# Stage 1 of a spectral mixing kernel: from one contraction over 128 rows to four row tiles of 32

## The chip, the cores and the metric

The kernel runs on one core of a Trainium2 chip. The metric is the device time in microseconds (us) of one execution; lower is better. The time of before is the median of three runs.

## The reference

Two global filters work on one image and a gate mixes them. The image `x` is 2048 rows by 1024 columns in bf16; each filter has weights for the real and the imaginary part, 2048 by 513.

```python
def _A_ref(x, w_r, w_i):
    B, S, D = x.shape                       # 1, 2048, 1024
    X = jnp.fft.rfft2(x.astype(jnp.float32), axes=(-2, -1))
    X = X * (w_r + 1j * w_i)
    return jnp.fft.irfft2(X, s=(S, D), axes=(-2, -1)).astype(jnp.bfloat16)
...
x = A_x
g = _sigmoid((x * gate_w).sum(-1, keepdims=True))
a = _A_ref(x, A_w_r, A_w_i)
b = _B_ref(x, B_w_r, B_w_i)
return g * a + (1 - g) * b
```

Both filters read the same `x`, so the forward transform is made once.

## The kernel before

The Fourier transforms are written as matrix products with constant tables, split so that each fits TensorE. The 2048 row indices are written as 64 n1 + 16 b + r, with n1 from 0 to 31, b from 0 to 3 (the residue that the change speaks of) and r from 0 to 15.

**Loads.** `x` is loaded with partition p holding the 16 rows 16 p to 16 p + 15, so partition p is 4 n1 + b and r is a place along the free dimension. Row blocks c = 0 to 3 hold four r each. `XPARTS` cuts them into nine DMAs: block 0 into one, one and two rows per partition, the others into two and two. All are issued on SP's queue, in order; two of the three loads of the table `M` stand between them (after blocks 0 and 1), the first `M` load goes by ACT's queue. Behind them, on SP's queue too, stand the table `F2`, the gate's weights (`GR`, eight rows of 128), `CK`, `SM`, and then all filter weights `w`, in six groups (w0 to w5; 44 DMAs with rows of 513 elements), and then `CL`, the tables for stage 5. The order within a queue is the order of the program text; every engine takes its own instructions in that order, and the class `Prog` turns the named reads and writes into semaphore waits.

**Fold.** VectorE adds and subtracts mirrored columns of x (`fold`, line 348) into `XF`, which holds two row blocks at a time.

**Stage 1** (`stage1`, matmul on line 387) is the first half of the transform down the columns. For each r, each half h, j and s there is one matmul with the folded x as the stationary operand and 256 columns of `M` (and of its negative, which `negate` writes on ACT or VectorE, lines 365 and 367) as the moving one. A column of M belongs to one b only, so three quarters of the table are zeros. The sums of one (h, j) of a row block fill two PSUM banks; they are evicted into `FT` by ACT (line 398) or, for two of them, VectorE (line 396), 1024 elements per partition at a time, for four r in a row.

**Stages 2 to 4**, for 16 steps: `fold3` on VectorE (line 443), the transform along the rows (`stage2`, lines 456 and 465), its eviction (line 471), the second half of the transform down the columns (`stage4`, line 482), its eviction (line 490), a DMA that swaps real and imaginary rows (`swap`), and the products with `w` on VectorE (`product`, line 505). The gate's spectrum is formed in between (line 518). **Stage 5** (line 614) and **stages 6 and 7** (lines 755 and 785) are the transforms back, with the gate, and the stores.

## Time and profile before

| | |
|---|---|
| time, median of 3 runs | 122.04 us (122.02 to 122.52) |
| the profiled execution | 122.14 us, span of its instructions 120.1 us |
| mean granted TensorE clock | 0.996 |
| TensorE busy | 114.1 us, 95% of the span |
| VectorE busy | 99.5 us, 83% |
| ACT busy | 99.0 us, 82% |
| DMA | 26.11 MB, 217 GB/s over the span |
| stage 1 matmuls, L387 | 128, starting from 5.0 to 20.3 us |
| stage 1 evictions on ACT, L398 | 15, starting from 8.3 to 21.1 us |
| stage 5 matmuls, L614 | 512, from 49.8 us on |

The page gives each engine's busy time; a matmul's end is modelled, so TensorE's share says little by itself. In the DMA row each digit is the busy share of the 16 DMA engines in one fortieth of the span. The chain of waits leads back from the last instruction to what released each step. In timelines a row is: start, duration, engine, line, operation, out<-in with shapes, count, and in brackets the idle time before it with what ended it.

### The profile page before, as it was taken

The page shows a single profiled execution, that of the slowest core. Times are in us where ns is not written, and L with a number is a line of the kernel's source. Part 1 is how long each engine was busy: PE and PEld are TensorE (multiplying, and loading weights), DVE is VectorE, ACT ScalarE, POOL GpSimd, SP SyncE. Part 2 cuts the span into 40 slices and gives each one's busy share as a digit, 9 for nine tenths or more (in the row PEclk, how much of TensorE's full clock was granted, in tenths as well). Part 3 has the DMA queues.
Part 4 walks back from the last instruction along what each step waited for, and adds up shares of the span by engine and source line. Part 5 has one row for each costly group of instructions (what it writes and reads, how often), then busy time and mean ns, then how long its engine had stood idle before and what let it go on. Part 6 is the DMA issues. An engine that isn't in the chain of part 4 may idle for free.

```text
span 120.1 us, 3690 instructions
## 1 busy us (share of the span) xinstructions
PE 114.1 (95%) x1556; PEld 95.9 (80%) x1556; DVE 99.5 (83%) x160; ACT 99.0 (82%) x119; POOL 38.4 (32%) x47
## 2 busy tenths in 40 slices
PE   6998999999999999999999999999999999999960
PEld 4676889787675675689999999999899979898630
DVE  0568999988999999999999949995695687787890
ACT  4249998999797999899999989999779868867710
POOL 1000010036575500000000000000029999999980
PEclk9999999999999999999999999999999999999998
DMA  2999999999999999832699500000000422434456
GB/s 84 328 394 421 415 331 366 349 350 352 361 369 364 360 370 368 321 137 85 162 392 394 199 0 5 0 5 0 0 5 8 158 96 93 175 124 160 160 222 215
DMA packets 17680, 26.11 MB, mean 217 GB/s; under 512 B 2112, under 2 KB 11072, under 8 KB 17664
## 3 DMA queue, kind: packets, MB, share of 16 engines
q1 hardware_dynamic: 16368, 23.00, 54.6%
q0 software_dynamic: 864, 2.36, 5.4%
q10 hardware_dynamic: 432, 0.52, 1.4%
q8 instruction: 12, 0.20, 0.7%
q14 instruction: 4, 0.03, 0.1%
HBM read 17.48 MB, written 4.19 MB: 180 GB/s over the span
## 4 chain that ended last, share of the span: by engine, by line
PE 59%; SPq 18%; DMA 9%; DVE 8%; issue 3%; ACT 1%; POOL 0%; DVEq 0%; POOLq 0%
PE PS L614 26%; SPq L290 18%; PE PS L785 14%; PE PS L755 11%; DMA WA<-in_B_w_i_dram 9%; DVE WA L505 3%; PE PS L304 3%; DVE WB L505 3%; PE PS L387 2%; DVE WA L796 1%; PE PS L561 1%; PE PS L482 1%; PE PS L588 1%; ACT WB L625 1%; DVEq L867 0%
## 5 line engine op out<-in xcount | busy, mean ns | idle before, releaser
L837 POOL TENSOR_TENSOR WA<-WA 128x512 bf16<-128x512 f32 x22 | 27.6, 1290 | 48.2 <-DVE WA L832 48.2
L614 PE MATMUL PS<-CL,WB 128*128 128x128 bf16 x256 | 31.8, 226 | 0.0
L614 PE MATMUL PS<-CL,WA 128*128 128x128 bf16 x256 | 31.7, 223 | 0.1
L614 PEld LDWEIGHTS PS<-CL,WB 128*128 128x128 bf16 x256 | 31.3, 145 | 0.3 <-DVE WB L505 0.2
L614 PEld LDWEIGHTS PS<-CL,WA 128*128 128x128 bf16 x256 | 31.3, 145 | 0.3 <-DVE WA L505 0.2
L625 ACT ACTIVATE WB<-PS 128x1024 bf16<-128x1024 f32 (+1 forms) x31 | 28.8, 1042 | 0.2 <-PE PS L614 0.2
L770 ACT ACTIVATE WA<-PS 128x1024 bf16<-128x1024 f32 (+1 forms) x16 | 15.8, 996 | 6.2 <-PE PS L755 6.1
L505 DVE TENSOR_TENSOR WB<-XF,WA 128x2048 bf16<-128x2048 bf16 (+2 forms) x14 | 19.3, 1384 | 1.0 <-ACT XF L490 0.5
L785 PE MATMUL PS<-FT,WA 128*128 128x256 bf16 (+1 forms) x132 | 19.3, 292 | 0.1
L505 DVE TENSOR_TENSOR WA<-MM,WA 128x2048 bf16<-128x2048 bf16 (+2 forms) x14 | 19.2, 1385 | 0.0
L482 PE MATMUL PS<-XF,CK 128*128 128x512 bf16 (+1 forms) x72 | 17.5, 356 | 0.2 <-ACT XF L490 0.2
L832 DVE TENSOR_TENSOR WA<-PS,WA 128x512 f32<-128x512 f32 x22 | 14.2, 686 | 4.2 <-PE PS L755 1.9
L471 ACT ACTIVATE XF<-PS 128x1024 bf16<-128x1024 f32 x16 | 16.7, 1052 | 1.1 <-PE PS L465 1.0
L490 ACT ACTIVATE XF<-PS 128x1024 bf16<-128x1024 f32 x14 | 14.7, 1050 | 1.4 <-PE PS L482 0.6
L387 PE MATMUL PS<-MM,XF 128*128 128x256 bf16 x128 | 15.4, 280 | 0.3 <-DVE XF L348 0.3
L387 PEld LDWEIGHTS PS<-MM,XF 128*128 128x128 bf16 x128 | 12.5, 100 | 3.3 <-DVE XF L348 1.4
L785 PEld LDWEIGHTS PS<-FT,WA 128*128 128x128 bf16 x132 | 12.3, 98 | 3.3 <-DVE WA L768 0.2
L290 POOL DMA_DIRECT2D MM<-XF x18 | 9.9, 550 | 14.3 <-PE PS L482 8.7
L398 ACT ACTIVATE FT<-PS 128x1024 bf16<-128x1024 f32 (+2 forms) x15 | 13.1, 1012 | 0.9 <-PE PS L387 0.9
L348 DVE TENSOR_TENSOR XF<-WB 128x512 bf16<-128x512 bf16 (+1 forms) x20 | 6.0, 366 | 5.9 <-DMA WB<-in_A_x_dram 5.9
L456 PEld LDWEIGHTS PS<-F,FT 128*128 128x128 bf16 x128 | 8.4, 98 | 3.1 <-ACT FT L398 0.2
L456 PE MATMUL PS<-F,FT 128*128 128x128 bf16 x128 | 10.2, 219 | 0.0
(77 smaller groups left out, 134.1 us busy)
## 6 DMA issues: line engine op xcount, KB each, us to landing
out_dram<-WA SPq DMA_DIRECT2D x14, 256.0 KB, 2.2
MM<-XF POOLq DMA_DIRECT2D x18, 128.0 KB, 5.3
WA<-in_A_x_dram SPq DMA_DIRECT2D x4, 512.0 KB, 8.3
FT<-c_U SPq DMA_DIRECT2D x1, 2048.0 KB, 8.5
MM<-XF SPq DMA_DIRECT2D x14, 128.0 KB, 3.2
WB<-in_A_x_dram SPq DMA_DIRECT2D x3, 512.0 KB, 5.9
WA<-in_A_w_r_dram SPq DMA_DIRECT2D x4, 256.5 KB, 5.8
WA<-in_A_w_i_dram SPq DMA_DIRECT2D x4, 256.5 KB, 6.2
```

Of the source, the lines that this page charges most:

```text
L290: return P.add(eng, lambda e: e.dma_start(dst, src), dma=name, **kw)
L387: P.add("pe", lambda e, o=o, lh=lh, rh=rh, s=s: e.matmul(o, lh, rh, start=(s == 0), stop=(s == 1)), r=[("xf", c % 2, q, h, s ^ j), ("M", c ...
L456: P.add("pe", lambda e, o=o, cs=cs, j=j, t=t, rh=rh: e.matmul(o, fblock(1 + cs, j, t), rh, start=(j == 0), stop=(j == 1)), r=[("F1a" if p ...
L471: P.add("act", lambda e: e.activation(dst, src, ACT.Copy), **kw)
L482: P.add("pe", lambda e, o=o, kind=kind, pm=pm, m=m, rh=rh: e.matmul(o, sl(CK, fbo(kind, pm, m), [(1, 128)]), rh, start=(m == 0), stop=(m = ...
L490: P.add("act", lambda e: e.activation(dst, src, ACT.Copy), **kw)
L505: P.add("dve", lambda e: e.tensor_tensor(out=at(sw), in0=sl(xt, xo + 64 * h0, [(0, 2), (128, 8 * ni), (1, 64 * n)]), in1=at(1), op=ALU.mul ...
L614: P.add("pe", lambda e, o=o, l0=l0, ab=ab: e.matmul(o, sl(WT[ab], l0, [(RWS[ab] // 2, 128)]), sl(CL, KIo[ab], [(1, 128)]), start=(ab == 0) ...
L625: P.add("act", lambda e: e.activation(dst, src, ACT.Copy), r=b, a=keys)
L770: P.add("act", lambda e, s=src, d=dst: e.activation(d, s, ACT.Copy), **kw)
L785: P.add("pe", lambda e: e.matmul(ps(col, [(1, n * 256)]), lh, rh, start=(k == 0), stop=(k == last)), r=[("Y", r), "DI"] + ["DJ"] * (full o ...
L837: P.add("pool", lambda e, s=s, op=op: e.tensor_tensor(out=ods(s, 0, 2), in0=pv[:, :, 0, :], in1=pv[:, :, 1, :], op=op), r=[("PQ", pk, 0), ...
```

## The change

The table `M` is stored without its zeros, [128, 512] in place of [128, 2048], with the four residues b as four groups of 32 partitions. The loads of x follow: partition 32 b + n1 now holds the rows 64 n1 + 16 b + r, so the source pattern of each load has a dimension of 4 outside one of 32. The nine DMAs keep their sizes and order; M is one DMA on ACT's queue and one negation on ACT.

A matmul of stage 1 then contracts over 32 partitions, with 64 moving columns, and there are four of them (g = 0 to 3), each in its own 32 rows of TensorE and its own PSUM bank, where one stood. A call of `stage1` fills four banks and evicts them in two evictions of 1024 elements. Row block 0 is evicted for two r at a time, with both h; the others for four r, one h at a time. The early key `F1a` goes, so `fold3` and `stage2` wait for `F1`.

```diff
-    C["M"] = M.reshape(128, 2048)
+    C["M"] = M.sum(-1).swapaxes(0, 1).reshape(128, 512)
...
-    xv = x2.rearrange("(p r) d -> p (r d)", r=16)
+    xsrc = lambda r, n: AP(x2.tensor, x2.offset + r * D, [[16 * D, 4], [64 * D, 32], [1, n * D]])
...
-    mload("act", 0, 1)
+    load("M", MM, 0, 512, cst["M"].ap(), eng="act", w=["M"])
     for c in range(4):
         t, o = xloc(c)
         for q0, n in XPARTS[c]:
-            dma("sp", f"x{c}{q0}", sl(t, o + q0 * 1024, [(1, n * 1024)]), xv[:, (4 * c + q0) * 1024:(4 * c + q0 + n) * 1024], w=[("x", c, q0)])
-        if c < 2:
-            mload("sp", 1 + c, 1 + c)
+            dma("sp", f"x{c}{q0}", sl(t, o + q0 * 1024, [(1, n * 1024)]), xsrc(4 * c + q0, n), w=[("x", c, q0)])
...
+    P.add("act", lambda e: e.activation(sl(MM, 512, [(1, 512)]), sl(MM, 0, [(1, 512)]), ACT.Copy, scale=-1.0), r=["M"], w=["NM"])
...
+    def stage1(c, q0, nq, hs, engs):
+
         nonlocal cnt
+        s0 = 4 * (cnt % 2)
+        cnt += 1
+        w = 128 * len(hs)
+        for q in range(q0, q0 + nq):
+            for h in hs:
                 for j in range(2):
+                    for s in range(2):
+                        for g in range(4):
+                            lh = sl(XF, (c % 2) * 4096 + q * 1024 + h * 512 + 256 * s + 128 * j, [(1, 128)], p0=32 * g, np_=32)
+                            rh = sl(MM, (4 * c + q) * 32, [(512 * s, 2), (1, 32)], p0=32 * g, np_=32)
+                            o = ps((s0 + g) * 512 + (q - q0) * w + (h - hs[0]) * 128 + j * 32, [(64, 2), (1, 32)])
                             P.add("pe", lambda e, o=o, lh=lh, rh=rh, s=s: e.matmul(o, lh, rh, start=(s == 0), stop=(s == 1)),
+                                  r=[("xf", c % 2, q, h, s ^ j), "M", "NM"], w=[bank(s0 + g)])
+        for g, eng in zip((0, 2), engs):
+            src = ps((s0 + g) * 512, [(512, 2), (1, w), (w, nq)])
+            dst = sl(FT, hs[0] * 8192 + 16 * g + 4 * c + q0, [(16, 2), (64, w), (1, nq)])
...
-    negate(0)
-    negate(1)
     folds(0)
     folds(1)
-    negate(2, 2, "dve")
-    stage1(0)
-    stage1(1)
+    for q0 in (0, 2):
+        stage1(0, q0, 2, (0, 1), ("act", "act"))
+    for hh in range(2):
+        stage1(1, 0, 4, (hh,), ("act", "act"))
...
-    stage1(2)
-    stage1(3)
+    for hh in range(2):
+        stage1(2, 0, 4, (hh,), ("act", "act"))
+    for hh in range(2):
+        stage1(3, 0, 4, (hh,), ("act", "dve"))
```

More of the change, by code (lines that the diff above doesn't have):

```diff
@@ L305, in bass_gated_mix__spectral_gfnet__spectral_gfnet__prompt_kernel @@
               r=["GRz"], w=[bank(7)])
-    def mload(eng, c0, n):
-        load(f"M{c0}", MM, c0 * 512, n * 512, cst["M"].ap()[:, c0 * 512:(c0 + n) * 512], eng=eng, w=[("M", c) for c in range(c0, c0 + n)])
-    mload("act", 0, 1)
+    load("M", MM, 0, 512, cst["M"].ap(), eng="act", w=["M"])
     for c in range(4):
@@ L359, in folds @@
             fold(c, q0, n, h)
-    def negate(c, n=1, eng="act"):
-        dst, src = sl(MM, 2048 + c * 512, [(1, n * 512)]), sl(MM, c * 512, [(1, n * 512)])
-        kw = dict(r=[("M", k) for k in range(c, c + n)], w=[("NM", k) for k in range(c, c + n)])
-        if eng == "dve":
-            P.add("dve", lambda e: e.tensor_scalar(out=dst, in0=src, scalar1=-1.0, scalar2=None, op0=ALU.mult), **kw)
-        else:
-            P.add("act", lambda e: e.activation(dst, src, ACT.Copy, scale=-1.0), **kw)
+    P.add("act", lambda e: e.activation(sl(MM, 512, [(1, 512)]), sl(MM, 0, [(1, 512)]), ACT.Copy, scale=-1.0), r=["M"], w=["NM"])
@@ L369, in bass_gated_mix__spectral_gfnet__spectral_gfnet__prompt_kernel @@
     cnt = 0
-    def stage1(c):
+    def stage1(c, q0, nq, hs, engs):
         nonlocal cnt
-        us = [(cnt + k) % 4 for k in range(4)]
-        cnt += 4
-        parts = XPARTS[c] if c == 0 else ((0, 4),)
-        for q0, n in parts:
-            for h in range(2):
-                for j in range(2):
-                    u = us[2 * h + j]
-                    for q in range(q0, q0 + n):
-                        r = 4 * c + q
-                        base = (c % 2) * 4096 + q * 1024 + h * 512
-                        o = ps(u * 1024 + q * 256, [(1, 256)])
-                        for s in range(2):
-                            lh = sl(XF, base + 256 * s + 128 * j, [(1, 128)])
-                            rh = sl(MM, r * 128, [(2048 * s, 2), (1, 128)])
-                            P.add("pe", lambda e, o=o, lh=lh, rh=rh, s=s: e.matmul(o, lh, rh, start=(s == 0), stop=(s == 1)),
-                                  r=[("xf", c % 2, q, h, s ^ j), ("M", c), ("NM", c)], w=[bank(2 * u + q // 2)])
-                    if q0 + n < 4:
-                        continue
-                    for m0, mn in ((0, 32), (32, 96)) if (c, h, j) == (3, 1, 1) else ((0, 128),):
-                        src = ps(u * 1024 + m0, [(128, 2), (1, mn), (256, 4)])
-                        dst = sl(FT, h * 8192 + j * 2048 + 16 * m0 + 4 * c, [(4096, 2), (16, mn), (1, 4)])
-                        kw = dict(r=[bank(2 * u), bank(2 * u + 1)], a=[("F1", h, j)] + [("F1a", h, j)] * (m0 == 0))
-                        if (c, h, j) in ((2, 1, 1), (3, 0, 1)):
-                            P.add("dve", lambda e, s=src, d=dst: e.tensor_copy(d, s), **kw)
-                        else:
-                            P.add("act", lambda e, s=src, d=dst: e.activation(d, s, ACT.Copy), **kw)
@@ new lines, in stage1 @@
+        for g, eng in zip((0, 2), engs):
+            src = ps((s0 + g) * 512, [(512, 2), (1, w), (w, nq)])
+            dst = sl(FT, hs[0] * 8192 + 16 * g + 4 * c + q0, [(16, 2), (64, w), (1, nq)])
+            kw = dict(r=[bank(s0 + g), bank(s0 + g + 1)], a=[("F1", h, j) for h in hs for j in range(2)])
+            if eng == "dve":
+                P.add("dve", lambda e, s=src, d=dst: e.tensor_copy(d, s), **kw)
+            else:
+                P.add("act", lambda e, s=src, d=dst: e.activation(d, s, ACT.Copy), **kw)
@@ L443, in fold3 @@
             P.add("dve", lambda e, dst=dst, src=src, op=op: e.tensor_tensor(out=dst, in0=src[0], in1=src[1], op=op),
-                  r=[("F1a" if i < 2 else "F1", cs, j) for cs in css for j in range(2)] + [("FR", i, j) for j in range(2)],
+                  r=[("F1", cs, j) for cs in css for j in range(2)] + [("FR", i, j) for j in range(2)],
                   w=[("E", i, cs, s) for cs in css] + [("FR", i - 2, s)] * (i > 1), a=["VD"] * (i == 1))
@@ L456, in stage2 @@
                         P.add("pe", lambda e, o=o, cs=cs, j=j, t=t, rh=rh: e.matmul(o, fblock(1 + cs, j, t), rh, start=(j == 0), stop=(j == 1)),
-                              r=[("F1a" if p < 2 else "F1", cs, j), "F2"], w=[bank(b0 + t % 2)])
+                              r=[("F1", cs, j), "F2"], w=[bank(b0 + t % 2)])
         if 1 in ab:
```

## The prediction, made before the changed kernel ran

> **What bounds the kernel now.** I read the page first, for where the transfers are dense, then the chain of waits, then the timelines of VectorE and TensorE for the first 50 us, and last the list of DMAs.

> ```profile
> DMA  2999999999999999832699500000000422434456
> GB/s 84 328 394 421 415 331 366 349 350 352 361 369 364 360 370 368 321 137 85 162 392 394 199 0 5 0 5 0 0 5 8 158 96 93 175 124 160 160 222 215
> ```

> A slice is 3.0 us. From the second slice to the fifteenth (3 to 45 us) the 16 DMA engines have no free time. Whatever holds up a transfer there holds up all that are queued behind it. The chain of waits leads through that stretch:

> ```profile
> 30.23 10.42 DMA WA<-in_B_w_i_dram
> 40.65 0.03 issue
> 40.68 0.02 DVEq L224
> 40.70 0.04 issue
> 40.74 1.61 DVE WB L505
> ```

> Before 30.23 us the chain runs through SP's queue, issue after issue (the w loads). So the filter weights (w, in six groups w0 to w5) set the pace up to 40.7 us. VectorE meets them just as they land:

> ```profile
> 31.24 2.38 DVE L505 TENSOR_TENSOR WB<-XF,WA 128x2048 bf16<-128x2048 bf16 x2 [0.26 <-DMA WA<-in_B_w_i_dram]
> ...
> 40.74 2.31 DVE L505 TENSOR_TENSOR WB<-XF,WA 128x4096 bf16<-128x4096 bf16 x1 [0.17 <-DMA WA<-in_B_w_i_dram]
> ```

> The first wait is for w2 (landed 31.14 us), the second for w3 (40.65 us). Slack at both is a fraction of a microsecond, and VectorE then works without a gap until stage 5. So a later w stream moves the end one for one. Ahead of w in SP's queue lie the nine loads of x:

> ```profile
> WA<-in_A_x_dram SPq DMA_DIRECT2D x4, 512.0 KB, 8.3
> WB<-in_A_x_dram SPq DMA_DIRECT2D x3, 512.0 KB, 5.9
> WB<-in_A_x_dram SPq DMA_DIRECT2D x2, 256.0 KB, 3.8
> ...
> CL<-in_gate_w_dram SPq DMA_DIRECT2D x1, 2.0 KB
> SM<-c_SM SPq DMA_DIRECT2D x1, 2.0 KB, 11.2
> ```

> **The change, part by part.**

> *The loads of x.* Before, 128 partitions are the first dimension. The new source pattern is [[16 D, 4], [64 D, 32], [1, n D]]: the first dimension counts 4, and its strides can't be merged with the second. Two rows bear on its price. By x's own rows of before it stays on 16 engines and costs nothing. By GR's row it goes to as many engines as the first dimension counts: four. I take GR's, as it is the row with a short first dimension. [...]

> Price on four engines: the packets of x take 159 ns for 4096 bytes (the median and the 1st percentile of 896, so it is the engine's own pace), 84 ns for 2048 bytes. A load of 128 rows of 4096 bytes is 8 packets per engine now (1.27 us; the trace has these landings 1.28 us apart) and 32 then (5.09 us): 3.82 us more, seven times, 26.7 us. The two loads of 2048-byte rows: 24 more packets of 84 ns, 2.02 us each, 4.0 us. Together 30.7 us.

> *The constants.* M shrinks from 512 KB to 128 KB; two loads leave SP's queue: per engine 8 packets of 46 ns and 8 of 84 ns, 1.04 us less. SP also saves 0.43 and 0.49 us of issue time, ahead of everything behind it; the engines, not SP, pace the queue, so I count nothing.

> Net delay of the queue behind x: 30.7 - 1.04 = 29.7 us. The last part of x lands at 15.58 + 29.7 = 45.3 us, w2 at 60.8, w3 at 70.3 us. Nothing recovers it on those four engines: the DMA share is 1.02 to 1.10 in every stretch from 4.4 to 50 us, and the w packets are at 47 to 48 ns from the 1st percentile to the median, so they run no faster in better company.

> *Stage 1 on TensorE.* 128 matmuls of 256 columns at 109 ns (14.0 us) become 512 of 64 columns with K = 32, each with its own weight load. No row has K = 32. Bounds from rows with a weight load each:

> ```profile
> 24.49 0.40 PE L465 MATMUL PS<-F,FT 128*128 128x64 bf16 x8
> 24.72 0.19 PE L518 MATMUL PS<-CK,VD 128*128 128x2 bf16 x2
> 24.77 0.24 PE L518 MATMUL PS<-CK,FT 128*128 128x2 bf16 x4
> 24.88 0.24 PE L518 MATMUL PS<-CK,VD 128*128 128x2 bf16 x4
> ```

> Eight of 64 columns start within 0.23 us (29 ns each), four of 2 columns within 0.105 us (26 ns). So 13.3 to 14.8 us, and at the pace of L614's 128-column pairs (61 ns) 31 us. I take 29 ns, the row of the same width: 14.8 us. Four tiles at once could also make it shorter. [...] In my forecast either is hidden: x comes in loads 5.09 us apart, each with 64 pairs, 1.9 us. Only what follows the last load counts.

> *Negation and evictions.* ACT loses one negation (0.63 us), VectorE one (0.42 us), both under the waits for x. 15 ACT and 2 VectorE evictions become 14 and 2. ACT's copies of 1024 elements all have means of 1.02 to 1.08 us whatever the pattern, so I give the pairs of the first block the same. Each set of four banks is evicted after its last matmul only; the next set of banks is free meanwhile, so TensorE waits for nothing.

> *The path through stage 1.* Last x at 45.3; six folds of 0.34 us, 47.4; the last 32 pairs at 29 ns, 48.4; eviction on VectorE 1.22 us, 49.6; fold3 and the first stage 2 up to ACT's first L471 about 0.9 us, 50.5 us. Before it was 22.08 us: 28.4 us later. The w path is 29.7 us later and ends last, at w2 and again at w3; the loads of CL behind w5 move by the same.

> Sum: the profiled execution took 122.14 us (span 120.1), 0.1 above the median of 122.04; 122.14 + 29.7 = 151.8 us.

> Bounds of this case: downward, if VectorE finds slack at w2 and w3 and the stage-1 path sets the end, 150.5; with its folds and evictions overlapped as well (3.3 us less), about 148. Upward, 61 ns a pair: after the last load 96 pairs are left (32 of the first half, 64 of the second), 5.9 instead of 2.8 us, and in part at the pace of the first matmuls of the trace (418 against 273 ns, though the granted clock reads 1.00), since TensorE idles over 2 us between loads: 154 to 157.

> **The rivals.**

> *x keeps 16 engines* (faster). For it: x's own rows. Against it: GR. The queue is then 1.04 us earlier, VectorE's two waits for w (0.43 us) vanish, and stage 1 runs from 0.7 us shorter to 0.8 us longer: 122.14 less 0.9 or so, 121.2, and up to 0.8 us more, 122.0. It decides if the loads of x show 16 landing events and the last lands before 16 us. Tiles that truly overlap would leave ACT as the bound (14 times 0.90 us): about 120.7.

> *Four engines, but other four for each load.* Loads would run side by side: the first complete block lands at 8 to 10 us in place of 6.9, the last of x about 2 us late: 124.5. For it speaks no row; GR is one DMA.

> *16 engines and pairs at 61 ns.* Stage 1 then takes 31 us in place of 14: 139 us. L465's 29 ns speaks against it.

> **Chances.** Four engines throughout: 0.85. 16 engines: 0.08 (0.05 faster, 0.03 within 0.5%, about what a measurement of this kernel can tell from no change). Rotating engines 0.04, slow pairs 0.03, both slower. Slower in all 0.92. The range 148 to 157 us is the likeliest case with its bounds; it holds about 0.93 of that case's 0.85, so 0.8.

> **What would show it.** In the list of DMAs the x loads lose their landing figure, as GR has none now, and show five events where 16 stood. GB/s falls to about 100 over the first 45 us (4 x 4096 bytes per 159 ns), at a quarter of the DMA share. VectorE's folds L348 wait for x some 25 us in all; matmuls of stage 1 come in bursts about 5 us apart and end near 48 us; VectorE's products wait for w until about 61 and 70 us; from stage 5 on the timeline is that of before, 29 to 30 us later. I am wrong if the x landings stay 1.3 us apart.

## The result and the profile after

The changed kernel takes 155.65 us (median of 4 runs, 155.12 to 156.34), the kernel before 122.07 us beside it: a ratio of 1.2744, 95% interval 1.2686 to 1.2802. The forecast was 151.8 us in a range of 148 to 157: right in sign and about the four engines, 3.85 us short, and wrong about the path that ends last. The profiled execution took 156.34 us with a span of 154.3 us, 34.2 us more than the 120.1 before. (Ratios leave disturbed runs out, so one can differ from the quotient of two medians.)

The page of after, busy share of the DMA engines, their rate, and the granted clock of TensorE, in slices of 3.86 us:

```profile
PEclk9955555555555557999999999999999999999999
DMA  2222222264458999999984428940000003243347
GB/s 48 85 105 106 108 106 104 108 169 146 153 170 221 282 314 345 362 362 365 366 329 175 142 74 271 395 154 4 0 4 0 4 2 134 106 170 132 144 166 244
```

For 31 us two tenths of the DMA engines are busy and move 105 GB/s. That is four engines of sixteen. The list of DMAs has lost its landing figures for x, as the prediction said:

```profile
WA<-in_A_x_dram SPq DMA_DIRECT2D x4, 512.0 KB
WB<-in_A_x_dram SPq DMA_DIRECT2D x3, 512.0 KB
WB<-in_A_x_dram SPq DMA_DIRECT2D x2, 256.0 KB
```

Each of these loads has five landing events: an early one, and four when data land. VectorE's timeline, each row with the wait ahead of it in brackets, shows what that does to the folds (now line 343) and to the first product with w (line 490):

```profile
24.91 2.10 DVE L343 TENSOR_TENSOR XF<-WB 128x512 bf16<-128x512 bf16 x6 [4.24 <-DMA WB<-in_A_x_dram]
30.00 0.76 DVE L343 TENSOR_TENSOR XF<-WA 128x512 bf16<-128x512 bf16 x2 [2.98 <-DMA WA<-in_A_x_dram]
36.71 1.96 DVE L343 TENSOR_TENSOR XF<-WA 128x512 bf16<-128x512 bf16 x4 [5.96 <-DMA WA<-in_A_x_dram]
42.19 0.76 DVE L343 TENSOR_TENSOR XF<-WA 128x512 bf16<-128x512 bf16 x2 [3.51 <-DMA WA<-in_A_x_dram]
48.69 2.21 DVE L343 TENSOR_TENSOR XF<-WA 128x512 bf16<-128x512 bf16 x6 [5.74 <-DMA WA<-in_A_x_dram]
...
59.27 1.23 DVE L490 TENSOR_TENSOR WB<-XF,WA 128x2048 bf16<-128x2048 bf16 x1 [1.82 <-ACT XF L475]
...
75.06 2.30 DVE L490 TENSOR_TENSOR WB<-XF,WA 128x4096 bf16<-128x4096 bf16 x1
```

The loads of 512 KB land 5.0 to 5.2 us apart up to 30 us, then 6.7, 5.5 and 6.5 us apart. The last one lands at 48.67 us, not at 45.3. And no product waits for w: the first waits for ACT, and the product that waited for w3 before follows its predecessor without a gap. The chain of waits says the same:

```profile
48.69 0.04 DVE XF L343
...
49.03 1.86 DVE XF L343 x5
50.89 1.19 DVE FT L380 x2
52.09 0.99 issue
53.08 0.28 DVE EO L428
53.37 0.05 issue
53.41 0.54 PE PS L450 x4
...
56.45 1.73 PE PS L467 x8
```

From x it goes through folds, the last evictions, fold3 and stage 2: the path through stage 1, not SP's queue of w. The delay along it, before against after:

| | before | after | later by |
|---|---|---|---|
| last x landed | 15.58 us | 48.67 us | 33.1 us |
| first eviction of stage 2 (L471, now L456) | 22.08 us | 54.80 us | 32.7 us |
| first product | 25.30 us | 59.27 us | 34.0 us |
| the product of w3 | 40.74 us | 75.06 us | 34.3 us |
| span | 120.1 us | 154.3 us | 34.2 us |

The rows of before for the first eviction of stage 2 and the first product:

```profile
22.08 1.94 ACT L471 ACTIVATE XF<-PS 128x1024 bf16<-128x1024 f32 x2
25.30 1.23 DVE L505 TENSOR_TENSOR WB<-XF,WA 128x2048 bf16<-128x2048 bf16 x1 [0.50 <-ACT XF L490]
```

So nearly the whole loss, 33.1 of 34.2 us, is there when x has landed.

### The profile page after: what moved, and what is told of

Read it like the earlier page. It is cut to its first block, busy times and chain, and to the rows that moved or that the text cites. A ratio compares the mean times of both kernels' runs of the same rounds, so it can differ in the third digit from the quotient of the medians.

```text
span 154.3 us, 4453 instructions
## 1 busy us (share of the span) xinstructions
PE 113.7 (74%) x1940; PEld 94.2 (61%) x1940; DVE 99.1 (64%) x159; ACT 99.1 (64%) x117; POOL 38.3 (25%) x47
## 4 chain that ended last, share of the span: by engine, by line
PE 61%; DMA 18%; SPq 13%; DVE 3%; issue 1%; ACT 1%; DVEq 0%
PE PS L599 20%; DMA WA<-in_A_x_dram 18%; SPq L290 13%; PE PS L770 11%; PE PS L467 10%; PE PS L740 9%; PE PS L441 5%; PE PS L450 3%; PE PS L503 2%; DVE XF L343 1%; DVE WA L781 1%; DVE FT L380 1%; ACT XF L475 1%; PE PS L546 1%; PE PS L573 0%
## 5 line engine op out<-in xcount | busy, mean ns | idle before, releaser
L373 PE MATMUL PS<-MM,XF 32*128 32x64 bf16 x512 | 12.6, 230 | 33.8 <-DVE XF L343 32.9
L382 ACT ACTIVATE FT<-PS 128x1024 bf16<-128x1024 f32 x14 | 13.6, 1024 | 35.6 <-PE PS L373 35.6
L373 PEld LDWEIGHTS PS<-MM,XF 32*128 32x128 bf16 x512 | 8.9, 114 | 37.8 <-DVE XF L343 37.2
L343 DVE TENSOR_TENSOR XF<-WB 128x512 bf16<-128x512 bf16 (+1 forms) x20 | 6.1, 367 | 20.9 <-DMA WB<-in_A_x_dram 20.9
L456 ACT ACTIVATE XF<-PS 128x1024 bf16<-128x1024 f32 x16 | 16.8, 1050 | 3.7 <-PE PS L450 3.4
L467 PE MATMUL PS<-XF,CK 128*128 128x512 bf16 (+1 forms) x72 | 18.3, 372 | 0.2 <-ACT XF L475 0.2
L343 DVE TENSOR_TENSOR XF<-WA 128x512 bf16<-128x512 bf16 (+1 forms) x14 | 5.7, 464 | 18.2 <-DMA WA<-in_A_x_dram 18.2
## 6 DMA issues: line engine op xcount, KB each, us to landing
out_dram<-WA SPq DMA_DIRECT2D x14, 256.0 KB, 2.1
WA<-in_A_x_dram SPq DMA_DIRECT2D x4, 512.0 KB
WB<-in_A_x_dram SPq DMA_DIRECT2D x3, 512.0 KB
```

The lines of the kernel that those rows point to most:

```text
L373: P.add("pe", lambda e, o=o, lh=lh, rh=rh, s=s: e.matmul(o, lh, rh, start=(s == 0), stop=(s == 1)), r=[("xf", c % 2, q, h, s ^ j), "M", "N ...
L456: P.add("act", lambda e: e.activation(dst, src, ACT.Copy), **kw)
L467: P.add("pe", lambda e, o=o, kind=kind, pm=pm, m=m, rh=rh: e.matmul(o, sl(CK, fbo(kind, pm, m), [(1, 128)]), rh, start=(m == 0), stop=(m = ...
```

## Experiments

The theory: the four engines of the source pattern make the whole loss, and x came 3.4 us later than forecast because the other twelve engines moved on to the next loads. Rivals: the 1024 small instructions of TensorE, its half clock, the evictions. Where a single run is named below, there is one execution and so no interval.

### The source pattern alone

The kernel before, with its 128-row matmuls and M with zeros:

```diff
-    C["M"] = M.reshape(128, 2048)
+    C["M"] = M.reshape(32, 4, 2048).swapaxes(0, 1).reshape(128, 2048)
-    xv = x2.rearrange("(p r) d -> p (r d)", r=16)
+    xsrc = lambda r, n: AP(x2.tensor, x2.offset + r * D, [[16 * D, 4], [64 * D, 32], [1, n * D]])
...
```

> The kernel before with one thing of the change: the source pattern of the x loads, 4 outside 32, with the rows of M (its zeros kept) put in the same order. Stage 1 contracts over 128 partitions as before. Theory (the loads run on four engines and that alone makes the loss): the x loads show five landing events each, the last lands at 45 to 50 us, and the time is 154 to 160 us, not below the changed kernel's, since 28 matmuls of 256 columns are left after the last load, about 6 us at half clock. Rival (the row tiles and evictions make a good part of the loss): the time is clearly below the changed kernel's 155.6, 125 to 150 us.

Measured: 156.59 us in a single run, five landing events a load, last x at 49.09 us. The pattern alone costs as much as the whole change, so beside it everything else in the change nets to about nothing (what the rest costs by itself comes below).

### What slows x after 30 us

In after, packets of 4096 bytes of x take 159 to 160 ns up to 32 us (32 of them make the 5.1 us), and 199 ns on average from 32 to 48 us; SP is done issuing the load of `F2` at 31.8 us. This run keeps `F2` and all behind it back until x has landed:

```diff
-    load("F2", F2, 0, 1536, cst["F2"].ap(), w=["F2"])
+    load("F2", F2, 0, 1536, cst["F2"].ap(), w=["F2"], r=[("x", 3, 2)])
```

> The changed kernel, with the load of F2, and so all that stands behind it in SP's queue, held until the last x has landed. It asks why the last x landed at 48.7 us and not at the 45.3 us of the prediction. Theory (the packets of x take 224 to 267 ns in place of 159 ns while the other twelve engines move other data): with nothing beside them all 4096-byte packets take 159 ns and the last x lands at 45 to 46 us; F2 and w then follow on 16 engines, the first w lands at about 51 us as it did, and the time falls by 1 to 3 us although the loads are held back. Rival (the four engines slow down by themselves): the last x lands at 48 to 49 us again and the time is the same or longer.

Measured: 159.12 us in a single run. The packets that took 199 ns after 32 us take 161 ns on average here, and the last x lands at 45.26 us, where the prediction had it (45.3). So it is the transfers behind x that slow it. The gain in time failed: w now starts late, and VectorE waits for it at two places, for w1 and for w2 (the prediction had w2 and w3 for the changed kernel):

```profile
59.97 1.23 DVE L490 TENSOR_TENSOR WB<-XF,WA 128x2048 bf16<-128x2048 bf16 x1 [6.02 <-DMA WA<-in_B_w_i_dram]
...
68.50 2.38 DVE L490 TENSOR_TENSOR WB<-XF,WA 128x2048 bf16<-128x2048 bf16 x2 [3.40 <-DMA WA<-in_B_w_i_dram]
```

So the transfers that slow x also bring w in time; 3.4 us of x is what they cost.

### Eight engines

Is it the count of the first dimension, or the number 4 and its stride? The kernel before, with rows in eight groups:

```diff
-    C["M"] = M.reshape(128, 2048)
+    C["M"] = M.reshape(16, 8, 2048).swapaxes(0, 1).reshape(128, 2048)
-    xv = x2.rearrange("(p r) d -> p (r d)", r=16)
+    xsrc = lambda r, n: AP(x2.tensor, x2.offset + r * D, [[16 * D, 8], [128 * D, 16], [1, n * D]])
...
```

> The kernel before, with the rows of x loaded by a source pattern whose first dimension counts 8, [[16 D, 8], [128 D, 16], [1, n D]], and the rows of M put in the same order. Theory (the engines used are as many as the first dimension counts, here 8): 9 landing events a load, 16 in place of 8 packets for each engine, so 7 times 1.27 us and 2 times 0.67 us later: last x at 25.8 us in place of 15.58, and 131 to 134 us in all. Rival (only the short dimension of 4 or the 64 D stride is what costs): 16 events, last x at 16 us, 122 to 123 us.

Measured: nine landing events a load, so eight engines: here too the first dimension is the number of engines. The time is 138.42 us in a single run, 4 us over the range, and the last x lands at 32.36 us, not 25.8. Packets averaged 223 ns from 6 to 21 us, most of it before `F2` or w ran, and 184 ns after. So the traffic of those later loads isn't the main cause here. What the cause is stays open.

### Sixteen engines by four DMAs of 32 partitions

```diff
-    dma("sp", ..., sl(t, o + q0 * 1024, [(1, n * 1024)]), xsrc(4 * c + q0, n))
+    for g in range(4):
+        dma("sp", ..., sl(t, o + q0 * 1024, [(1, n * 1024)], p0=32 * g, np_=32), xsrc(4 * c + q0, n, g))
```

> The changed kernel with each of the nine x loads issued as four DMAs, one for each residue, 32 partitions each, so that the first dimension counts 32 (36 DMAs on SP's queue). Theory: every x DMA shows 16 landing events; SP needs some 0.42 us for each, so the last x lands at about 17.5 us and the weights w up to 2 us later than before; time 120.5 to 124 us. Rival (row tiles cost by themselves): over 125 us.

Measured: 134.75 us, ratio 1.1034 (1.0990 to 1.1078). All sixteen events are back, and 20.9 of 33.6 us are recovered, but the last x lands at 24.01 us, not near 15. The packets are slow: 276 ns at the median for 4096 bytes in place of 159. The last of the 36 DMAs, 0.46 us each to issue, is issued at 17.8 us, so issue isn't the limit. From 6.6 to 19.8 us the engines move 236 GB/s; before's page has up to 421. The chain of waits of this run goes through w, which stands behind the slow loads: the product of w3 starts at 52.78 us, 12.0 us later than before, as the span is 11.9 us longer.

Whether the packets are slow because only 32 partitions are written at a time was a guess, shown by no run so far. Two runs that issue from two queues (28 DMAs) ask it. The first writes to both halves of the partitions at a time, the second to one half at a time:

```diff
+            for k, (eng, g) in enumerate((("sp", 0), ("act", 2), ("sp", 1), ("act", 3))):
+                dma(eng, ..., p0=32 * g, np_=32), xsrc(4 * c + q0, n, g), ...)
...
+            for k, (eng, g) in enumerate((("sp", 0), ("act", 1), ("sp", 2), ("act", 3))):
```

> The changed kernel with each x load cut by residue into DMAs of 32 partitions, issued from two queues at once: residues 0 and 1 (partitions 0 to 63) from SP, 2 and 3 (64 to 127) from ACT; row blocks 2 and 3 are loaded whole, so 28 DMAs, 14 on each queue; the negation of M moves to VectorE. In the split run each 4096-byte packet took 276 ns at the median and x came at 236 GB/s. Theory (the loads of the split run were slow because only 32 neighbouring partitions were written at a time): the packets take 159 to 190 ns, x comes at about 400 GB/s, the last x lands at 15 to 17 us, and the time is 119.5 to 123 us. Rival (a DMA to 32 partitions is slow whatever runs beside it): packets near 276 ns, the last x at 22 to 24 us, 131 to 135 us.

> The run with two queues, with the residues in another order: SP issues residues 0 and 2, ACT 1 and 3, so that the two queues are at work in the same half of the partitions (0 to 63, then 64 to 127). Theory (writes to one half of the partitions share their way in): packets at 270 to 320 ns, the last x at 21 to 24 us, time 129 to 135 us. Rival (two queues are enough, wherever they write): as with the halves apart, the last x at 15 to 17 us and 119.5 to 123 us.

Measured: both halves 135.11 us (ratio 1.0945, 1.0878 to 1.1012); the same half 136.97 us in a single run. From 6 to 20 us the 4096-byte packets average 204 ns with both halves and 242 ns in the same half, but the engines move 283 and 266 GB/s, only 6% apart, and the last x lands at 21.26 and 21.40 us. Neither theory came out: with both halves neither 159 to 190 ns nor 400 GB/s, with one half not the 270 to 320 ns. The halves make little difference to x, so the partitions written are not shown to be what slows these DMAs; the cause stays open.

x lands 2.8 us earlier than in the split run, and yet little time is gained: by the ratios 1.1 us, with intervals that overlap. The reason stands in TensorE's timeline of the run with both halves:

```profile
16.64 1.14 PE L376 MATMUL PS<-MM,XF 32*128 32x64 bf16 x52 [2.10 <-issue]
23.79 1.78 PE L376 MATMUL PS<-MM,XF 32*128 32x64 bf16 x117 [2.61 <-issue]
29.85 0.93 PE L376 MATMUL PS<-MM,XF 32*128 32x64 bf16 x54 [2.83 <-issue]
```

"issue" means that the engine waited for nothing that the profile names. The three waits are 7.5 us, and the chain of waits goes through them; in the split run, whose x came later, they were 0.2 us. These rows begin at TensorE's instructions 450, 706 and 962 (matmuls, weight loads and its few waits for semaphores counted together), 256 apart. The instruction queue (q8) has packets of 16384 bytes; they land at 15.32, 22.28 and 28.43 us, and TensorE goes on 1.3 to 1.5 us after each. The pages of before, after and the last run below (512 fewer instructions of TensorE than after) show whose they are:

```profile
q8 instruction: 12, 0.20, 0.7%
q8 instruction: 15, 0.25, 0.7%
q8 instruction: 13, 0.21, 0.7%
```

The first figure counts packets. After has 768 more instructions of TensorE than before and three more packets, so a packet brings 256 of them. I read the waits as TensorE out of instructions.

### 128-row matmuls with the same loads, and wider ones

The first run has before's stage 1 (256 instructions of TensorE in place of 1024) behind the two-queue loads; the second has the four row tiles with each moving column taken twice, so that stage 1's result isn't the reference's.

```diff
-    C["M"] = M.reshape(128, 2048)
+    C["M"] = M.reshape(32, 4, 2048).swapaxes(0, 1).reshape(128, 2048)
...
-                            rh = sl(MM, (4 * c + q) * 32, [(512 * s, 2), (1, 32)], p0=32 * g, np_=32)
+                            rh = sl(MM, (4 * c + q) * 32, [(512 * s, 2), (0, 2), (1, 32)], p0=32 * g, np_=32)
```

> The kernel before with the loads of the two-queue run (halves apart) and the rows of M, its zeros kept, in the same order: stage 1 contracts over 128 partitions as before. Beside the two-queue run it asks what row tiles, the smaller M and the new evictions are worth when the loads don't differ. Theory (four row tiles at once take 12 ns a pair where the full rows take 27 for the same work, and M is 384 KB smaller): 0.5 to 2.5 us slower than the two-queue run, 121 to 125 us. Rival (stage 1 is set by ACT's evictions and VectorE's folds, so the tiles bring nothing): within 0.5 us of it.

> The two-queue run (halves apart) with 128 moving columns in place of 64 in each stage 1 matmul: each column of M goes in twice and the sums of j = 0 and j = 1 go to the same place, so stage 1's result is not that of the reference. It asks what sets the pace of the row tiles. In the changed kernel a group of four took 52 ns at half clock in its steady stretches. Theory (the tiles run side by side and the columns set the pace): a group of four takes twice as long, about 105 ns at half clock or 55 at full. Rival (issue sets the pace): 52 ns a group again.

Measured: full rows 131.31 us, ratio 1.0703 (1.0654 to 1.0752). That is about 3 us faster than the halves run by the ratios (0.0242 of 122.5 us), though its x lands later (22.56 us): against expectation the old stage 1 (its matmuls, its larger M and its evictions together) is the better one here. No wait is named issue. Wide: 135.73 us in a single run, with issue waits of 6.4 us in place of 7.5. In its steady stretches at half clock groups of four start 107 ns apart, with 64 columns 53 ns, so the four tiles overlap and their time goes by columns; but twice the columns left the end where it was: the run with both halves lies between 133.2 and 136.0 us. So it is not the time of the matmuls that sets the end.

### The change without its source pattern

Here the changed kernel reads x as before did. Rows then lie in another order than stage 1 takes them, so only its durations mean something.

```diff
-    xsrc = lambda r, n: AP(x2.tensor, x2.offset + r * D, [[16 * D, 4], [64 * D, 32], [1, n * D]])
+    xv = x2.rearrange("(p r) d -> p (r d)", r=16)
```

> The changed kernel with the x loads' source as before (128 partitions as the first dimension): the rows then lie in another order than stage 1 takes them, so its result is not the reference's; every duration is that of the four row tiles, the small constants and the paired evictions alone. Theory (the source pattern makes the whole loss, the rest is worth what the prediction's case of 16 engines says): x lands by 15 us with 16 events a load, 120.5 to 122.0 us, faster than before by 0 to 1.5 us; the instruction fetches, which in the kernel with two queues of x started 5.3 us after TensorE's 194th instruction, start under 2.5 us after it with one queue, as before (1.8 us), and TensorE shows under 1 us of waits named issue. Rival (1024 in place of 256 instructions of TensorE in stage 1 are slow to come by whatever the queues): issue waits of 2 us and more at two or three places, 124 us or more.

Measured: 130.3 us, ratio 1.0638 (1.0580 to 1.0696). The last x lands at 15.70 us with 16 events, as before, and yet the kernel is 7.6 us slower: the rival. TensorE's timeline, and ACT's first eviction of stage 2:

```profile
13.75 2.67 PE L373 MATMUL PS<-MM,XF 32*128 32x64 bf16 x116 [1.51 <-issue]
...
19.73 1.78 PE L373 MATMUL PS<-MM,XF 32*128 32x64 bf16 x117 [1.70 <-issue]
...
25.26 0.93 PE L373 MATMUL PS<-MM,XF 32*128 32x64 bf16 x54 [2.29 <-issue]
```

```profile
29.16 1.02 ACT L456 ACTIVATE XF<-PS 128x1024 bf16<-128x1024 f32 x1 [1.84 <-PE PS L450]
```

The same instructions, 450, 706 and 962, and again 1.3 to 1.4 us behind a 16 KB packet. The first of these packets starts 3.8 us after TensorE's 194th instruction (expected: under 2.5). The eviction comes 7.1 us later than before (22.08 us), 5.5 us of it these three waits.

A last run keeps all of that and leaves out, of each sum of two products in stage 1, the second: 512 TensorE instructions are left.

```diff
-                    for s in range(2):
+                    for s in range(1):
...
+                            P.add("pe", lambda e, o=o, lh=lh, rh=rh, s=s: e.matmul(o, lh, rh, start=True, stop=True),
```

> The four row tiles on the x source of before, as in the run before this one (130.3 us), with the second of the two products of each sum in stage 1 left out: 256 pairs in place of 512, 512 TensorE instructions in place of 1024; the folds, the loads, the evictions and all that follows are the same (the numbers are not the reference's). Theory (the loss of that run is TensorE waiting for its instructions, 256 to a fetch, three times, 5.5 us): stage 1 now crosses one such border in place of three, its 450th instruction comes only after 14 us, by when the fetch started at its 194th has landed; issue waits under 1.5 us in all, the first copy of stage 2 (L456) at 22 to 24.5 us in place of 29.2, and 121.5 to 125 us in all. Rival (the half clock of TensorE, or evictions that wait for four banks at a time): stage 1 still ends late, L456 after 26 us, and over 126 us.

Measured: 123.57 us, ratio 1.0119 (1.0075 to 1.0163). The waits of TensorE, line, releaser, then us in total, times and longest:

```profile
PE PS L373 <- DVE XF L343: 4.9, 9, 1.2
PE PS L373 <- ACT FT L382: 2.5, 5, 0.6
PE PS L304 <- POOL DUM L302: 1.1, 1, 1.1
PE PS L450 <- DVE EO L428: 0.7, 1, 0.7
PE PS L467 <- ACT XF L475: 0.2, 1, 0.2
```

No matmul waits for issue any more (one weight load does, 0.5 us), the fetch lands at 13.55 us and the 450th instruction starts at 16.74 us. ACT now evicts without a pause and bounds stage 1:

```profile
8.99 11.30 ACT L382 ACTIVATE FT<-PS 128x1024 bf16<-128x1024 f32 x12 [0.68 <-PE PS L373]
...
22.09 1.02 ACT L456 ACTIVATE XF<-PS 128x1024 bf16<-128x1024 f32 x1 [1.72 <-PE PS L450]
```

The first eviction of stage 2 is back at 22.09 us (22.08 before), with the granted clock at 0.5 from 9.0 to 26.1 us. The theory holds: the number of instructions, not the clock and not the evictions, held TensorE in stage 1. What is left of the loss, 1.3 us of span, is there at the first product, which starts at 26.55 in place of 25.30 us.

### The clock

TensorE's record reads 0.5 from 8.2 to 59.4 us in after. This run has 24 matmuls of 256 columns, of no use, ahead of the last two loads' matmuls:

```diff
+            if (c, q, hs) == (3, 2, (0,)):
+                for _ in range(24):
+                    P.add("pe", lambda e: e.matmul(ps(4 * 512, [(1, 256)]), sl(MM, 0, [(1, 128)]), sl(MM, 0, [(1, 256)]), start=True, stop=True),
...
```

> The changed kernel, with 24 matmuls of 256 columns on data that is not used, placed in TensorE's order into the wait for the last x load. It asks what the granted clock of 0.5 from 8.2 to 59.4 us costs. Theory: the granted clock is back at 1.0 before the last x lands, the tail of stage 1 and the first steps of stages 2 to 4 run at full clock, and the time falls by 1.5 to 2.5 us, to 153 to 154. Rival (the half clock is hidden by ACT and VectorE): within 0.5 us of the changed kernel.

Measured: 155.32 us, ratio 1.2687 (1.2646 to 1.2729), not to be told from after. The clock went to 1.0 at 46.8 us, but back to 0.5 from 53.65 to 57.06 us. So the run tests the tail of stage 1, and there the rival is right: from the last x (48.20 us) to the first eviction of stage 2 (54.32 us) it took 6.1 us, nearly all of it at full clock, as after did at half clock. It doesn't test the first steps of stages 2 to 4, which began at half clock again; but the clock comes back within the first eight matmuls of stage 4. They start 213 ns apart up to 56.85 us and 109 ns apart from 57.07 us, and take 1.62 us (1.87 in after); from the first eviction of stage 2 to the first product it is 4.23 us (4.47 in after). So there the half clock does cost time.

## Why the prediction was right, and where it was short

**Four engines.** Right, and it was nearly the whole result: five events, 105 GB/s, loads 5.1 us apart, and 156.59 us by the pattern alone. The reading of `GR`'s nine events carried over to a 4 and to an 8.

**The price of a packet.** This is the term that was mis-sized. The sum took 159 ns for each 4096-byte packet and argued that "nothing recovers it", for the w packets run no faster in better company. It didn't ask the reverse: whether x runs slower in worse company. SP's queue goes on while x is under way, and the twelve idle engines start `F2`, `CK` and w, so the x packets took 199 ns on average from 32 us on. Last x at 48.67 in place of 45.3 us: 3.4 us. Without that traffic it is 45.26 us.

**Which path ends last.** Wrong. The sum had w2 at 60.8 and w3 at 70.3 us; they landed at 61.8 and 70.9 us, close enough. But the path through stage 1, forecast 1.3 us behind the w path (28.4 against 29.7), was the later one by far: 3.4 us of late x, 0.9 us more from the last x to the first eviction of stage 2 (54.80 us; 45.3 + 5.2 = 50.5 had been forecast, and it took 6.1 us after x), 1.25 us more from there to the first product (4.47 in place of 3.22 us), and 0.2 us from there on. 28.4 + 3.4 + 0.9 + 1.25 + 0.2 is the 34.2 us of the span. Of the 0.9 us, 0.8 is the term for fold3 and the first stage 2: the sum had 0.9 us, it took 1.7 us (53.08 to 54.80 us), and before's own rows have 1.7 us too (20.35 to 22.08 us). The 1.25 us goes with the half clock. TensorE runs the same matmuls there as before, without idle time in either kernel: stage 4's first eight took 1.87 us in place of 1.05, and the other 0.4 us lies in those of stage 2 ahead of them. The run of half the instructions, with 0.5 in the same place, has the same step (4.46 us) and no late x. Where the clock came back within these eight matmuls, in the run with useless matmuls (57.06 us) and in that with the plain source (32.02 us), they took 1.62 and 1.68 us and the step 4.23 and 4.28 us. The sum had no term for the clock on this path.

**The range.** That 155.65 us lies inside is in part luck. The stretch from 154 to 157 us stood for slow pairs after the last load; the pairs were fast, and late x filled their place. The lower end is also off in its own terms: 150.5 less 3.3 is 147.2, not 148.

**Stage 1 on TensorE.** Its 29 ns a pair was too long: in after four tiles start about 3 ns apart and a group of four takes 53 ns at half clock, 13 ns a pair. That four tiles at once could make it shorter was right: they do run side by side. The verdict "hidden" was right for the changed kernel, whose x comes so slowly that its instruction packets, at 16.7, 27.3 and 39.2 us, all land in time. The remark that the first matmuls of before take 418 ns "though the granted clock reads 1.00" misreads the record: its first entry is at 6.45 us, and what lies ahead counts as full clock (the page's first two digits are 9). Up to there these matmuls start 213 ns apart, from 6.47 us on 109 ns.

**The rival of 16 engines** would have failed where it mattered. It promised 121.2 us; with x on 16 engines the row tiles took 130.3 us. The bounds priced 512 pairs by how long TensorE takes to run them, from 13.3 to 31 us, and not by how long they take to arrive. What the prediction never counted is that 1024 instructions within 20 us cross three borders of 256. The row tiles would have lost time even with perfect loads.

**Negation, evictions.** Nothing in after, as forecast, and with half the instructions stage 2's first eviction comes when it did before; the 14 evictions on ACT take their old 0.9 to 1.0 us each. That TensorE waits for none of them holds only while x is slow: with x on 16 engines it waited 2.6 us for them, in five places (2.5 us with half the instructions).

**What would show it.** The lost landing figures, five events and the rate came out as written. The folds' waits for x were 39.1 us in all, not 25, and the products' waits for w never came.

## What to carry to other kernels

Count the first dimension of every DMA pattern before anything else: where it counted 4 or 8, that was the number of engines, read off in the landing events (five and nine: one early, one for each engine), and the price is the packets that each engine then gets in a row (32 of 159 ns with four engines, 5.1 us a load), plus what the idle engines' next transfers do to them (199 ns). Before cutting one matmul into many small ones, count TensorE's instructions against the time they have: they came 256 to a fetch, and TensorE stood still where the next 256 came late (5.5 us in three places, x on 16 engines). No version here beat the kernel before; keeping 128 partitions in one pattern and the old number of instructions was worth more here than a table without zeros.

## What the hardware did that was not expected

- DMAs to 32 partitions, on all 16 engines: 4096-byte packets at 276 ns (median), 236 GB/s, against 159 ns and up to 421 GB/s with 128 partitions. Not explained: writing to both halves of the partitions at a time gave 283 GB/s, to one half 266.
- Eight engines with 16 partitions each: 223 ns from 6 to 21 us, with four engines 160 ns. Not explained.
- Instruction fetches were the bound of TensorE in stage 1 where x came on 16 engines: packets of 16 KB took 0.9 to 1.7 us and started 0.9 us (after), 3.8 us (the plain source) and 5.3 us (two queues of x) after TensorE's 194th instruction. Why so different is open; the long ones came while the 16 engines were busy with x (DMA digits of 9 on both pages).
- Stage 1 by row tiles ran at half clock: with the plain source, x at full rate, the clock digits read 5 from 9.6 to 32 us, while the busy digits of TensorE's matmuls in stage 1 read 1 to 6.
